# Which score blocks a pair must have free tiles for, in a set-attention kernel followed by an MLP

## The chip, the cores and the metric

The kernel runs on one core of a Trainium2 chip. The metric is the device time of one execution in microseconds. A core has a matmul engine (PE, or TensorE), a vector engine (DVE), a scalar engine (ACT), GpSimd (POOL) and a sync engine (SP), which issues this kernel's DMA transfers. Each engine takes its instructions in the order in which the program issued them and waits on semaphores for what other engines have to deliver.

## The reference

Four batches of 12480 tokens with 128 channels go through an attention in two stages over 32 inducing points, and every token of the result then goes through an MLP of width 2048:

```python
def _attn_ref(x, inducing) -> np.ndarray:
...
    def mab(q, kv):
        s = scale * (q @ kv.transpose(0, 2, 1))
        s = s - s.max(-1, keepdims=True)
        a = np.exp(s)
        a /= a.sum(-1, keepdims=True) + 1e-09
        return a @ kv
    h = mab(I, x)
    return mab(x, h).astype(np.float32)
...
def _moe_ref(x, w_in, w_out) -> np.ndarray:
    h = x @ w_in
    g = h * (1.0 / (1.0 + np.exp(-1.702 * h)))
    return (g @ w_out).astype(np.float32)
```

The first `mab` needs all tokens of a batch before its 32 rows `h` are known. The second scores each token against `h`.

## The kernel before

**Tiling.** A batch is cut into seven parts: six whole super-blocks of 2048 tokens (s = 0 to 5), each of four blocks of 512, and a left-over of 192 tokens (s = 6), two groups of 96. The MLP takes its input block by block. The left-overs of two neighbouring batches make one block together, so there are 98 blocks: 24 of batch 0, one of the left-overs of batches 0 and 1, 24 of batch 1, and the same again for batches 2 and 3. A block has eight **steps** (NG = 8, each for 256 of the 2048 hidden units), 784 steps in all. The block of the first two left-overs begins at step 192, batch 1 at 200, batch 2 at 392, the second pair of left-overs at 584.

**The main loop** (lines 783 to 815) runs over these steps. `first(i)` (line 683) multiplies the stacked softmax weights `st` with `hw`, the product of `h` and `w_in`, into `ph`, and takes the gelu as a sum of two rounded parts, `hi` and `lo`. `second(i, c)` (line 710) multiplies these with the weights `wh` and `wl` into `pso`. The second products follow the first at a distance, `lag`, of 6 to 12 halves. The arithmetic between is on ACT (`g`, some of `hi`) and DVE (`lo`, the rest of `hi`).

**The attention beside it.** While the MLP works on batch b − 1, the attention of batch b is issued in small pieces between its steps. `attention(b)` (line 197) is a generator; the main loop calls `next(rest, None)` once at the end of each step (line 808), so each `yield` in it is a step of waiting. `hop(n)` yields n times, and from batch 1 on `wait(n)` is `hop(n)`, four times without a number. It goes as follows:

- First scores, `first_products` and `first_out`, in pairs of parts: (0, 1), (2, 3), (4, 5), and (6) alone (line 394).
- `maximum`, exponentials, their transposes `aT_of` and the weighted sum `weigh` over all seven parts, which loads the tokens again as `xn` and reloads `xt` for later (lines 405 to 430), then `hT`, the 32 rows (line 441).
- Second scores, `second_products` and `second_out`, in two turns (line 503). For batch 2 the turns are (0, 1), (2, 3) and then (4, 5), (6). For batches 1 and 3, whose left-over is needed first, they are (6, 0), (1, 2) and then (3, 4), (5). At the end of each turn stand its exponentials and `yield LUMP`. The loop answers LUMP by issuing second products until only six halves are held back.

`weights_of(b, s)` (line 534) turns the second exponentials into the stacked weights `st` for the blocks of a super-block, on DVE, POOL and by DMA. `lay_out` (line 775) starts it at a due step, 14 before the first block of the super-block, and earlier where the next one needs it (174 for the left-over of batch 1, 378 for the first super-block of batch 2, 566 for the left-over of batch 3). If the exponentials are not there by then, `lay_out` calls `next(rest)` over and over until they are.

`h_w_in` (line 519) makes `hw` for the next batch in four parts, at steps 186, 188, 190 and 193 for batch 1, 385, 387, 389 and 391 for batch 2, and 578, 580, 582 and 585 for batch 3. It uses the tag `pa`, two PSUM banks, as the scores do.

**The tiles that scores go to.** `take` (line 137) gives a whole super-block a tile from a ring of EB = 9 under tag `e`, for first and second scores alike, and writes `False` for it into the list `held`. A left-over gets a tile of a ring of its own, `e_last`, and no entry. `give_back` sets the entry to `True`: `aT_of` does so for first scores and `weights_of` for second scores. `full(n)` (line 133) asks, for each of the next n takes, whether the entry nine places back is still `False`. Before a pair the generator yields as long as `full(len(pair))` holds (lines 395 and 506). Each batch makes twelve entries: batch 0 has 0 to 5 for first scores and 6 to 11 for second, batch 1 has 12 to 17 and 18 to 23, batch 2 has 24 to 29 and 30 to 35, batch 3 has 36 to 41 and 42 to 47.

Of the kernel before, what the change touches and what calls it, by code (L numbers as in the profile page):

```python
# [55 lines left out]
def set_attention_then_moe(ctx: ExitStack, tc, xT, x, indT, w_in, w_out, outT):  # L56
# [31 lines left out]
    NS = len(sups)  # L88
    EB = NS + 2
# [40 lines left out]
    pace = [0]  # L130
    held = []

    def full(n=1):

        return any(len(held) + k >= EB and not held[len(held) + k - EB] for k in range(n))

    def take(name, s):
        if s == NS - 1:
# [9 lines left out]
    def hop(n=4):  # L148

        for _ in range(n):  # L150
            yield
# [7 lines left out]
    def load_xT(b, s):  # L159
        t0, g, w = sups[s]  # L160
        if g == G:
            t = px.tile([P, SUP], F32, tag="xt", name="xt")
        else:
            t = px.tile([P, g * w], F32, tag="xt_last", name="xt_last", bufs=1)
        nc.sync.dma_start(t[:, 0:g * w], xT[:, b * N + t0:b * N + t0 + g * w])
        xts[b, s] = t
# [30 lines left out]
    def attention(b):  # L197
# [15 lines left out]
        def first_products(s):  # L213
            t0, g, w = sups[s]
            pa = ps_a.tile([P, 512], F32, tag="pa", name="pa")
            xg = xts[b, s][:, 0:g * w]
            if start:
                xg = xg.rearrange("c (k g i) -> c g k i", g=g, i=32)
            else:
                xg = xg.rearrange("c (g t) -> c g t", g=g)  # L220
            for j in range(g):
                pe_.matmul(
                    pa[32 * j:32 * j + 32, 0:w], indT_sb, xg[:, j], start=True, stop=True
                )
            return pa

        def first_out(s, pa):
            t0, g, w = sups[s]
            q = 32 * g
            e, slot = take("s1", s)  # L230
            if start:
                act.copy(e[0:q, 0:w], pa[0:q, 0:w])
                dve.tensor_reduce(mx[0:q, s:s + 1], pa[0:q, 0:w], axis=AX.X, op=ALU.max)
            else:
                dve.tensor_copy(e[0:q, 0:w], pa[0:q, 0:w])
                dve.tensor_reduce(mx[0:q, s:s + 1], e[0:q, 0:w], axis=AX.X, op=ALU.max)
            s1[s] = e, slot
# [65 lines left out]
        def pairs(some):  # L303
            some = list(some)
            return [some[k:k + 2] for k in range(0, len(some), 2)]

        def again(s):

            if s < NS - 1:
                load_xT(b, s)  # L310
# [81 lines left out]
            dve.tensor_add(hu, hu, h2[:, 0:P])  # L392
        else:
            for pair in pairs(range(NS)):
                while full(len(pair)):
                    yield
                pas = [first_products(s) for s in pair]
                yield
                for s, pa in zip(pair, pas):
                    if s + XB < NS:  # L400
                        load_xT(b, s + XB)
                    first_out(s, pa)
                    yield from wait(2)
                yield from wait(2)
# [46 lines left out]
        def second_products(s):  # L451
            t0, g, w = sups[s]
            pa = ps_a.tile([P, 512], F32, tag="pa", name="pa")
            for j in range(g):
                pe_.matmul(
                    pa[32 * j:32 * j + 32, 0:w], hT[:, 0:M], xts[b, s][:, j * w:(j + 1) * w],
                    start=True, stop=True,
                )
            return pa

        def second_out(s, pa):

            t0, g, w = sups[s]
            q = 32 * g
            e, slot = take("e", s)
            k = w // 32
            e = e[:, 0:w].rearrange("p (k m) -> p k m", m=M)
            dve.transpose(e[0:q].rearrange("p k m -> p (k m)"), pa[0:q, 0:w])
            m2 = psm.tile([P, BLK], F32, tag="m2", name="m2")
            dve.tensor_reduce(m2[0:q, 0:k], e[0:q], axis=AX.X, op=ALU.max)  # L470
            yield
            eng = dve if start and s == 0 else nc.gpsimd
            eng.tensor_sub(e[0:q], e[0:q], m2[0:q, 0:k].unsqueeze(2).broadcast_to([q, k, M]))  # L473
            yield
            return e, slot

        def exponentials(s, e):
            q = 32 * sups[s][1]
            act.activation(e[0][0:q], e[0][0:q], AF.Exp, scale=scale)
            es[b, s] = e  # L480
# [22 lines left out]
        for some in (turn[2:],) if start else (turn[0:4], turn[4:]):  # L503
            yield from hop(20 if start else 8)
            for pair in pairs(some):
                while full(len(pair)):
                    yield
                pas = [second_products(s) for s in pair]
                yield
                for s, pa in zip(pair, pas):  # L510
                    if s + XB < NS:
                        again(s + XB)
                    mine[s] = yield from second_out(s, pa)
                yield from wait(2)
            for s in some:
                exponentials(s, mine[s])
            yield LUMP
# [214 lines left out]
    squared = [0]  # L732
    loaded_w = []
    att = attention(0)
    with tc.tile_pool(name="pf", bufs=FB) as pf, tc.tile_pool(name="pw", bufs=2) as pw:
        dec = weights()
# [13 lines left out]
    def attentions():  # L750
        yield from att
        for b in range(1, B):
            while first_block[b - 1, 0] * NG > now[0]:
                yield
            yield from attention(b)

    n = len(work) * NG
# [91 lines left out]
```

## Time and profile before

| | us |
|---|---|
| median of 3 runs | 1657.11 |
| lowest and highest | 1654.92, 1658.01 |
| the profiled execution | 1656.42 |
| its span, from the first to the last instruction | 1654.6 |

The profile is of that one execution. Its page lists busy time by engine, the span in 40 slices, the DMA queues, the chain of work that ended last, and the costliest groups of instructions. Nearly all compute instructions have line 46, the helper that records them, so one goes by the tiles' names: `pa` for scores and small products, `ph` for the first products, `pso` for the second, `e` and `s` for score tiles, `xt` and `xn` for loaded tokens. In the timeline a row has start, duration, engine, line, operation, output and inputs, and in brackets the idle time before it and what ended that. Consecutive `ph` rows on PE mark the steps of the main loop.

### The profile page before, as it was taken

The numbers are of one execution on the slowest core, as the hardware profiler recorded it, in microseconds if no ns is written. First come the engines' busy times: TensorE is split into PE (matmuls) and PEld (weight loads), VectorE is DVE, ScalarE is ACT, GpSimd is POOL, SyncE is SP. The second block draws the span as 40 slices with busy tenths as digits, with TensorE's granted clock in tenths as the row PEclk, the third lists the DMA queues.
The fourth block names the chain that finished last, engine by engine and source line by source line (L and its number), as shares of the span: only waits on it lengthen the run. The fifth ranks groups of instructions, "written<-read, shape, count | busy, mean of one in ns | idle before, by whom it ended". The sixth has DMA issues, their size and how long they took to land.

```text
span 1654.6 us, 21847 instructions
## 1 busy us (share of the span) xinstructions
PE 1595.2 (96%) x7737; PEld 1239.9 (75%) x7737; DVE 1382.3 (84%) x1524; ACT 1326.1 (80%) x1504; POOL 189.8 (11%) x134
## 2 busy tenths in 40 slices
PE   5799999999989999999979999999999999999999
PEld 3577787777667877777747777777766888888887
DVE  7798987888769888788877988878888888888886
ACT  6488888988768888888757887898876988788885
POOL 4311110110301011011020110110122011001100
PEclk9799999999999999999999999999999999999999
DMA  8305102841141110374123201149210111011010
GB/s 333 103 21 189 42 25 58 191 107 51 60 145 70 39 45 26 69 187 98 45 71 133 87 19 39 45 91 217 52 66 22 37 45 42 17 45 45 20 45 20
DMA packets 81947, 126.66 MB, mean 77 GB/s; under 512 B 11632, under 2 KB 50096, under 8 KB 75696
## 3 DMA queue, kind: packets, MB, share of 16 engines
q1 hardware_dynamic: 81840, 125.26, 26.6%
q8 instruction: 63, 1.03, 0.3%
q14 instruction: 44, 0.36, 0.1%
HBM read 74.10 MB, written 25.56 MB: 60 GB/s over the span
## 4 chain that ended last, share of the span: by engine, by line
PE 89%; DVE 5%; ACT 2%; DMA 2%; issue 1%; POOL 1%; SPq 0%; ACTq 0%; DVEq 0%; POOLq 0%
PE pso L46 63%; PE ph L46 22%; PE pa L46 4%; DVE lo L46 2%; DMA xt<-in_xT 2%; DVE e L46 1%; DVE m L46 1%; ACT hi L46 1%; ACT g L46 1%; DVE hw L46 0%; DVE hi L46 0%; ACT L46 0%; DVE t L46 0%; ACT s L46 0%; DVE sm L46 0%
## 5 line engine op out<-in xcount | busy, mean ns | idle before, releaser
L46 DVE TENSOR_TENSOR lo<-g,hi 128x1024 fp32r<-128x1024 f32 (+1 forms) x784 | 976.2, 1256 | 154.2 <-ACT hi L46 141.3
L46 ACT ACTIVATE g<-ph 128x1024 f32<-128x1024 f32 (+1 forms) x784 | 805.1, 1030 | 245.8 <-PE ph L46 138.6
L46 PE MATMUL pso<-hi,wl 128*128 128x512 f32 (+1 forms) x1568 | 626.7, 400 | 0.0
L46 PE MATMUL pso<-hi,wh 128*128 128x512 f32 (+1 forms) x1568 | 618.9, 395 | 0.0
L46 PE MATMUL pso<-lo,wh 128*128 128x512 f32 (+1 forms) x1568 | 618.0, 394 | 0.0
L46 PE MATMUL ph<-st,hw 128*128 128x512 f32 x1536 | 490.9, 401 | 11.1 <-ACT g L46 8.9
L46 ACT ACTIVATE hi<-ph 128x1024 fp32r<-128x1024 f32 x455 | 465.2, 1022 | 0.0
L46 PEld LDWEIGHTS ph<-st,hw 128*128 128x128 f32 x1536 | 284.2, 189 | 99.3 <-issue 16.4
L46 PEld LDWEIGHTS pso<-lo,wh 128*128 128x128 f32 x1568 | 296.0, 189 | 73.0 <-issue 3.7
L46 PEld LDWEIGHTS pso<-hi,wl 128*128 128x128 f32 x1568 | 296.5, 189 | 71.3 <-issue 2.8
L46 PEld LDWEIGHTS pso<-hi,wh 128*128 128x128 f32 x1568 | 296.5, 189 | 70.6
L46 DVE CAST hi<-g 128x1024 fp32r<-128x1024 f32 (+1 forms) x329 | 242.2, 736 | 86.3 <-ACT g L46 85.6
L546 POOL TENSOR_TENSOR e<-e,sm 128x512 f32<-128x512 f32 (+1 forms) x27 | 39.1, 1448 | 1143.5 <-DVE sm L46 898.4
L46 ACT COPY ob<-pso 128x512 f32<-128x512 f32 (+1 forms) x98 | 57.8, 590 | 27.2 <-PE pso L46 27.2
L473 POOL TENSOR_TENSOR e<-e,m 128x512 f32<-128x512 f32 (+1 forms) x27 | 34.8, 1289 | 203.2 <-DVE m L46 203.2
L550 POOL TENSOR_TENSOR e<-e,ah 128x512 f32<-128x512 f32 (+1 forms) x27 | 49.7, 1841 | 2.2
L46 PE MATMUL pa<-xt,indT_sb 128*32 128x512 f32 x192 | 25.7, 638 | 15.9 <-DMA xt<-in_xT 15.9
L46 ACT ACT_TABLE_LOAD x28 | 35.9, 1283 | 4.4 <-issue 3.3
L549 POOL CAST ah<-e 128x512 fp32r<-128x512 f32 (+1 forms) x27 | 34.5, 1277 | 1.7
L46 PE MATMUL pa<-xt,hT 128*32 128x512 f32 x192 | 26.0, 639 | 7.2 <-DVE e L46 4.0
L46 ACT ACTIVATE e<-e 128x512 f32<-128x512 f32 (+1 forms) x28 | 15.2, 576 | 21.6 <-POOL e L473 14.0
L46 PE MATMUL pa<-w_in_sb,hT 128*128 128x512 f32 x24 | 14.0, 669 | 12.1 <-DVE hw L46 8.3
(97 smaller groups left out, 445.1 us busy)
## 6 DMA issues: line engine op xcount, KB each, us to landing
xt<-in_xT SPq DMA_DIRECT2D x48, 1024.0 KB, 7.1
out_T<-ob SPq DMA_DIRECT2D x96, 256.0 KB, 2.0
xn<-in_x SPq DMA_DIRECT2D x72, 256.0 KB, 7.0
st<-ahT SPq DMA_DIRECT2D x192, 64.0 KB, 2.0
st<-alT SPq DMA_DIRECT2D x192, 64.0 KB, 2.0
raw<-in_w_in SPq DMA_DIRECT2D x4, 512.0 KB, 8.9
raw<-in_w_out SPq DMA_DIRECT2D x4, 512.0 KB, 8.3
xt_last<-in_xT SPq DMA_DIRECT2D x4, 96.0 KB, 8.2
```

Of the source, the lines that this page charges most:

```text
L46: return f(*a, **k)
L473: eng.tensor_sub(e[0:q], e[0:q], m2[0:q, 0:k].unsqueeze(2).broadcast_to([q, k, M]))
L546: eng.tensor_mul(e[0:q], e[0:q], sm[0:q, 0:nb].unsqueeze(2).broadcast_to([q, nb, M]))
L549: eng.tensor_copy(ah[0:q, 0:w], e2[0:q])
L550: eng.tensor_sub(e2[0:q], e2[0:q], ah[0:q, 0:w].bitcast(F32))
```

## The change

`full` is given the parts of the pair instead of their number. It counts those that are whole super-blocks and looks at the entries nine places back for so many takes. A pair (6, 0) is asked about one tile instead of two, and (6) alone about none. Both calls, before first scores and before second scores, are changed alike.

```diff
-    def full(n=1):
-
-        return any(len(held) + k >= EB and not held[len(held) + k - EB] for k in range(n))
+    def full(some):
+
+        free = range(len(held) - EB, len(held) - EB + sum(s < NS - 1 for s in some))
+        return any(k >= 0 and not held[k] for k in free)
...
-                while full(len(pair)):
+                while full(pair):
                     yield
                 pas = [first_products(s) for s in pair]
...
-                while full(len(pair)):
+                while full(pair):
                     yield
                 pas = [second_products(s) for s in pair]
```

## The prediction

> **What bounds the kernel now.** I read the page first: the busy shares, then the chain of work that ended last.
>
> ```profile
> span 1654.6 us, 21847 instructions
> ...
> PE 1595.2 (96%) x7737; PEld 1239.9 (75%) x7737; DVE 1382.3 (84%) x1524; ACT 1326.1 (80%) x1504; POOL 189.8 (11%) x134
> ...
> PE 89%; DVE 5%; ACT 2%; DMA 2%; issue 1%; POOL 1%; SPq 0%; ACTq 0%; DVEq 0%; POOLq 0%
> ```
>
> TensorE is busy for 96% of the span and holds 89% of the chain. A change that only moves work can win no more than the time in which PE waits or runs slowly. So the question is where those places are, and whether the moved step touches them. The timeline of PE, followed along the first products (`ph<-st,hw`, one pair of them in each step of the main loop), gives the rhythm. Here are four stretches of it, each around an undisturbed step: a plain step, one with a part of `h_w_in`, one with a pair of scores, one with the left-over scores.
>
> ```profile
> 822.32 0.63 PE L46 MATMUL ph<-st,hw 128*128 128x512 f32 x2
> 824.26 1.92 PE L46 MATMUL pa<-xt,hT 128*32 128x512 f32 x16
> 826.11 0.74 PE L46 MATMUL ph<-st,hw 128*128 128x512 f32 x2
> 828.09 0.63 PE L46 MATMUL ph<-st,hw 128*128 128x512 f32 x2
> ...
> 849.75 0.63 PE L46 MATMUL ph<-st,hw 128*128 128x512 f32 x2
> 851.60 0.63 PE L46 MATMUL ph<-st,hw 128*128 128x512 f32 x2
> 852.07 1.02 PE L46 MATMUL pa<-w_in_sb,hT 128*128 128x512 f32 x2
> 854.31 0.63 PE L46 MATMUL ph<-st,hw 128*128 128x512 f32 x2
> ...
> 882.13 0.63 PE L46 MATMUL ph<-st,hw 128*128 128x512 f32 x2
> 884.09 0.36 PE L46 MATMUL pa<-xt_last,hT 128*32 128x96 f32 x4
> 884.38 0.74 PE L46 MATMUL ph<-st,hw 128*128 128x512 f32 x2
> ```
>
> A plain step lasts 851.60 − 849.75 = 1.85 us. A part of `h_w_in` makes it 2.71 (+0.86). A pair of scores takes 828.09 − 822.32 = 5.77 for two steps, 2.07 above two plain ones, so one whole super-block costs about 1.03. The left-over costs 2.25 − 1.85 = 0.40.
>
> Against these prices I set three stretches of the windows view, one for each of the batches 1, 2 and 3, around the second scores, and two quiet stretches below them. The columns are the stretch, its length, then busy time (and instructions) of PE, PEld, DVE, ACT and POOL, the granted clock, the DMA share and GB/s.
>
> ```profile
> 408.98:464.04 55.06, 48.03 (x211) 32.55 (x210) 43.94 (x54) 35.19 (x41) 15.64 (x13) 0.94 0.16 56
> 828.09:880.26 52.17, 39.88 (x161) 26.36 (x160) 36.74 (x42) 29.75 (x34) 12.15 (x9) 0.93 0.18 59
> 1219.38:1272.97 53.59, 46.60 (x211) 31.41 (x210) 43.53 (x54) 35.15 (x41) 15.64 (x13) 0.97 0.16 57
> 600.00:650.00 50.00, 50.00 (x216) 40.20 (x215) 42.96 (x44) 40.70 (x46) 4.91 (x3) 1.00 0.09 29
> 268.00:345.00 77.00, 77.00 (x441) 61.03 (x440) 60.73 (x63) 70.31 (x85) 5.24 (x3) 1.00 0.69 159
> ```
>
> PE stands idle 7.03, 12.29 and 6.99 us in the three, none in the quiet two, and the clock drops below 1.00 in the three alone. The real loss is larger than the idle time:
> Batch 1 runs 19 steps (35.15), the left-over (0.40), six whole super-blocks (6.2) and three parts of `h_w_in` (2.58), 44.3 in all. It took 55.06: **10.7 lost**.
> Batch 2 runs 15 steps (27.75), two pairs (4.14) and four parts (3.44), 35.3. It took 52.17: **16.8 lost**.
> Batch 3 is the work of batch 1, 44.3. It took 53.59: **9.3 lost**. Together 36.8 us.
>
> What the loss is made of, in the timeline of PE:
>
> ```profile
> 413.14 1.97 PE L46 MATMUL pa<-xt,hT 128*32 128x512 f32 x16 [1.00 <-DVE e L46]
> ...
> 421.72 1.22 PE L46 MATMUL ph<-st,hw 128*128 128x512 f32 x2 [2.70 <-ACT g L46]
> ...
> 454.45 0.73 PE L46 MATMUL ph<-st,hw 128*128 128x512 f32 x2
> 458.24 1.49 PE L46 MATMUL pa<-w_in_sb,hT 128*128 128x512 f32 x2 [3.05 <-DVE hw L46]
> 462.08 0.72 PE L46 MATMUL ph<-st,hw 128*128 128x512 f32 x2
> ...
> 860.10 0.73 PE L46 MATMUL ph<-st,hw 128*128 128x512 f32 x2
> 864.68 1.74 PE L46 MATMUL pa<-w_in_sb,hT 128*128 128x512 f32 x2 [3.85 <-DVE e L46]
> 868.64 0.62 PE L46 MATMUL ph<-st,hw 128*128 128x512 f32 x2
> ...
> 1232.10 0.73 PE L46 MATMUL ph<-st,hw 128*128 128x512 f32 x2 [2.70 <-ACT g L46]
> ...
> 1267.18 1.47 PE L46 MATMUL pa<-w_in_sb,hT 128*128 128x512 f32 x2 [3.05 <-DVE hw L46]
> ```
>
> There are two kinds. First a **burst**: at its due step `lay_out` calls `next(rest)` until the weights of the next batch exist, so both pairs, four `second_out` and the exponentials are issued at once (413.14, 421.72, 1232.10). Then a **collision**: the second turn of pairs, late too, shares the two `pa` banks with `h_w_in` (458.24, 864.68, 1267.18). Both come of one lateness.
>
> **The change, part by part.** Where the lateness comes from shows in two rows, the last first-score pair of batch 1 and its left-over:
>
> ```profile
> 182.19 1.92 PE L46 MATMUL pa<-xt,indT_sb 128*32 128x512 f32 x16
> ...
> 243.55 0.36 PE L46 MATMUL pa<-xt_last,indT_sb 128*32 128x96 f32 x4
> ```
>
> These are 61.4 us apart, 32 steps; the pair itself has 7 yields. For the other 25 steps the generator stands in `while full(len(pair))` for a tile that the left-over never takes. By the yields in the code: pair (4, 5) at step 56, left-over possible at 63; tile 18 − 9 = 9, that of super-block 3 of batch 0, comes back at step 87 (its weights are laid out 14 steps before its first step 96, and 5 steps later it is returned), so the left-over runs at 88. `hT` follows at 166, the second scores would begin at 175, and `lay_out` of (1, 6) is due at 174.
>
> *What is removed:* for a left-over alone the new `full` looks at no tile. Batch 1: 63, `hT` 141, pair (6, 0) at 150, pair (1, 2) at 157, exponentials at 164, ten steps ahead of 174; pair (3, 4) at 173, (5) at 180, done at 185, ahead of `h_w_in` at 186. Batch 2 goes from 288 to 263: pairs at 350 and 357, exponentials 364 (due 378), then 373, 380, done 385, when `h_w_in` starts. Batch 3 goes from 480 to 455 and repeats batch 1 (164 becomes 556, due 566). The bursts go, and the second turn no longer lies among the parts of `h_w_in`. I take the whole 36.8.
>
> *The rule for second scores itself* frees nothing: in the old order pair (6, 0) came at 174, when tile 10 was long back (119). In the new order tiles 10 and 11 are back at 119 and 151, and pair (1, 2) comes at 157; in batch 2 tile 23 is back at 351 and its pair comes at 357. Cost and gain zero, with six steps to spare.
>
> *What moves:* DVE, ACT, POOL and DMA work of batch b stays the same in number; it lies 25 steps (46 us) earlier beside the same steady loop. Three collections of exponentials, one a batch, now return LUMP to the main loop instead of having it swallowed inside `lay_out`, so the loop issues its six held-back halves behind them; these are no extra matmuls. The moved middle part (exponentials, `aT`, `weigh`, loads of `xn` and `xt`) now begins at step 80, just ahead of `weights_of` of super-block 3 at 82, which has DVE and POOL work of its own. Below, this costs nothing, as 268 to 345 has the same work beside super-block 4 with PE at 77.00 of 77.00. Above, it is bounded by a burst's wait each time, 2.70 and about 1.5 of slow clock, 12.6 for three batches. I take 2, near the lower end, because that row shows the very same work.
>
> *What is new:* attention of batch 3 ends seven steps earlier and so begins at step 392 instead of 399, at the first step of a super-block, when SP also issues the last four stack loads. Batch 2 begins at such a step now (200), and its second load comes late:
>
> ```profile
> 487.53 0.62 PE L46 MATMUL ph<-st,hw 128*128 128x512 f32 x2
> ...
> 492.10 1.09 PE L46 MATMUL pa<-xt,indT_sb 128*32 128x512 f32 x8 [2.26 <-DMA xt<-in_xT]
> 493.12 1.22 PE L46 MATMUL ph<-st,hw 128*128 128x512 f32 x2
> 496.58 0.63 PE L46 MATMUL ph<-st,hw 128*128 128x512 f32 x2
> ```
>
> 496.58 − 487.53 = 9.05 where a pair and two steps need 5.77: 3.3 lost. Batch 3 may take from 0 to 3.3; I take 3.3, as the queue has the same order there. Batch 2 keeps its own.
>
> The page "TensorE: Matmul & The Clock Gate" of the Trainium skill (Part 1) lets the clock fall only after an idle window of about 3.4 us. By that, the 2.26 us of the load would cost 2.3 and the sum would be an estimated 1 us better. The trace disagrees: after 2.70 idle the matmuls at 421.72 took 1.22 instead of 0.63, while after 2.70 at 1232.10 they took 0.73, so a shorter wait can cool the array or not.
>
> **Sum:** 36.8 − 2 − 3.3 = 31.5 us off the profiled execution's 1656.42 us (its span 1654.6 and 1.8 around it): 1624.9. That execution lay 0.7 below the median of 1657.11, so I say 1625.5.
>
> **Rivals.**
> *The collision stays.* If the LUMP at 185 or 385 holds ACT just as `h_w_in` needs its copies, the waits at 458.24, 864.68 and 1267.18 remain: 462.08 − 454.45 = 7.63 against 2.71, 4.9 lost, about the same in batch 3, and 868.64 − 860.10 = 8.54 against 2.71, 5.8; 15.6 in all. Saved 36.8 − 15.6 − 3.3 = 17.9: 1639. For it: the two still follow each other closely. Against: with no pair between them, each part of `h_w_in` waits for the bank of the part two before it, four steps old.
> *A larger gain.* The load waits of batches 2 and 3 both vanish and nothing is paid: 36.8 + 3.3 = 40.1, 1617.
> *Nothing changes.* If the second pairs waited instead, for tiles 11 or 23, until step 174 or 378, the bursts would stay: 1657. The spare six steps speak against it.
> *Slower.* SP is one queue in order. The stacks of super-block 3 (steps 90 to 96) now stand behind the moved loads:
>
> ```profile
> xt<-in_xT SPq DMA_DIRECT2D x48, 1024.0 KB, 7.1
> ...
> xn<-in_x SPq DMA_DIRECT2D x72, 256.0 KB, 7.0
> ```
>
> If a stack had to wait for one of each, PE would miss it for 14.1 us and 1.6 of slow clock, 47 for three batches: 47 + 3.3 − 36.8 = 13.5 slower, 1671. It decides from a delay of 11.2 us a batch. Against: the row 268 to 345 has the same loads beside the stacks of super-block 4, DMA share 0.69, and PE never idle.
>
> **How the numbers follow.** Forecast 0.68, with 1618 to 1636 as its own range (the two unknown costs at their ends give 1620 to 1636). Collision stays 0.14 (1636 to 1645). Larger gain 0.08. Nothing 0.04. Slower 0.06. The range 1615 to 1642 takes in the forecast, half of the larger gain and most of the staying collision, 0.82. About 0.2% (3.3 us) is what a measurement of this kernel can tell from no change. Faster is 0.68 + 0.14 + 0.08 = 0.90, same 0.04, slower 0.06.
>
> **What would show it.** In the changed trace the left-over's first scores of batch 1 should start about 13 us after their pair, not 61; the pairs of second scores should lie seven steps apart, each in a step of 3.8 us; the waits of 2.70 for `g` and 3.05 and 3.85 for `hw` and `e` should be gone; a wait for `xt` should stand at step 396. I am wrong if PE waits for `hw` after the LUMP, for `lo` in steps 80 to 96, or for a stack at a step that is a multiple of eight.

## The result, and the profile after

| | median us | lowest to highest | ratio to before, with its 95% interval |
|---|---|---|---|
| before | 1657.56 | 1654.92 to 1659.52 | |
| after | 1632.13 | 1632.03 to 1632.70 | 0.9848, 0.9831 to 0.9865 |

The change makes the kernel 25.4 us faster. The forecast was 1625.5, with a range of 1615 to 1642. The profiled execution after took 1632.70 us. Its page, with the rows that answer to those of before:

```profile
span 1630.9 us, 21863 instructions
...
PE 1591.0 (98%) x7737; PEld 1233.0 (76%) x7737; DVE 1386.9 (85%) x1515; ACT 1331.5 (82%) x1513; POOL 197.9 (12%) x134
```

PE does the same 7737 matmuls and is busy for 98% of a span that is 23.7 us shorter. The busy time itself fell by only 4.2 us, so most of the gain is waiting that went away. The place of it shows when both traces are cut at the same steps. The cuts must lie where the same work is done on either side, so each stretch runs from before the last first scores of a batch to behind its second scores and the first pairs of the next one. Here are windows of the trace before, from step 50 to 250, 250 to 442, 442 to 608 and 620 to 780 (columns as in the prediction):

```profile
170.49:578.10 407.61, 398.30 (x1929) 310.56 (x1928) 342.91 (x379) 334.19 (x378) 43.51 (x31) 0.99 0.29 80
578.10:978.92 400.82, 388.02 (x1855) 298.25 (x1854) 331.68 (x356) 322.56 (x362) 37.22 (x25) 0.99 0.30 80
978.92:1316.34 337.42, 330.22 (x1631) 257.69 (x1630) 282.99 (x314) 279.08 (x318) 38.36 (x28) 0.99 0.28 71
1338.58:1635.11 296.53, 296.53 (x1281) 240.25 (x1280) 256.95 (x255) 244.24 (x266) 19.78 (x12) 1.00 0.12 35
```

The same four stretches of steps after the change:

```profile
170.50:572.70 402.20, 397.97 (x1930) 308.71 (x1928) 343.36 (x375) 336.76 (x381) 45.64 (x31) 0.99 0.30 81
572.70:959.79 387.09, 384.26 (x1855) 296.26 (x1854) 333.67 (x353) 324.45 (x365) 40.97 (x25) 1.00 0.30 83
959.79:1290.27 330.48, 329.28 (x1631) 256.55 (x1630) 284.58 (x311) 280.93 (x321) 40.75 (x28) 1.00 0.29 72
1312.67:1611.34 298.67, 298.67 (x1282) 240.12 (x1280) 257.32 (x255) 244.22 (x266) 19.79 (x12) 1.00 0.12 35
```

The matmul counts agree to one, so the stretches hold the same work. At step 50 both kernels are at 170.5 us. Then the three stretches are 5.4, 13.7 and 6.9 us shorter, 26.1 in all; idle PE in them falls from 9.31, 12.80 and 7.20 us to 4.23, 2.83 and 1.20. From step 608 to the end the kernel takes 340.6 us instead of 338.3 (1630.9 − 1290.27 against 1654.6 − 1316.34): 2.4 come back in a tail whose work the change does not touch (see the rhythm of the tail below). The 26.1 and the 2.4 make the span's 23.7.

What the moved middle of batch 1 costs shows beside this. Both rows are the 64 steps that end with `hT`, first before, at steps 102 to 166, then after, at steps 77 to 141:

```profile
268.55:396.01 127.46, 127.46 (x718) 101.14 (x716) 105.59 (x116) 112.79 (x130) 12.35 (x8) 1.00 0.51 117
```

```profile
222.23:350.66 128.43, 128.29 (x717) 100.87 (x716) 106.71 (x115) 111.05 (x129) 9.89 (x6) 1.00 0.51 116
```

It is 0.97 us dearer at its new place. In batch 2 it is 0.89 (128.39 against 127.50), in batch 3 0.87 (128.38 against 127.51): 2.7 in all. In batch 1 the extra lies in steps 87 to 95.

The early left-over and the second scores that are no longer in a burst, in PE's timeline after:

```profile
197.23 0.36 PE L46 MATMUL pa<-xt_last,indT_sb 128*32 128x96 f32 x4
...
367.34 0.63 PE L46 MATMUL ph<-st,hw 128*128 128x512 f32 x2
...
369.47 1.03 PE L46 MATMUL pa<-xt,hT 128*32 128x512 f32 x6
370.43 0.74 PE L46 MATMUL ph<-st,hw 128*128 128x512 f32 x2
```

The left-over's first scores stand at 197.23 instead of 243.55. Pair (6, 0) of batch 1 is at step 150, alone, and its step lasts 370.43 − 367.34 = 3.09 us without a wait. The waits of 2.70 for `g`, of 3.05 for `hw` and of 3.85 for `e` are gone.

### The profile page after: what moved, and what is told of

Its sections match the earlier page's. It is cut to its first block, busy times and chain, and to the rows that moved or that the text cites. A ratio compares the mean times of both kernels' runs of the same rounds, so it can differ in the third digit from the quotient of the medians.

```text
span 1630.9 us, 21863 instructions
## 1 busy us (share of the span) xinstructions
PE 1591.0 (98%) x7737; PEld 1233.0 (76%) x7737; DVE 1386.9 (85%) x1515; ACT 1331.5 (82%) x1513; POOL 197.9 (12%) x134
## 4 chain that ended last, share of the span: by engine, by line
PE 88%; DVE 4%; ACT 3%; DMA 2%; issue 2%; SPq 1%; POOL 0%; ACTq 0%; DVEq 0%; POOLq 0%
PE pso L46 62%; PE ph L46 22%; PE pa L46 4%; DMA xt<-in_xT 2%; DVE lo L46 2%; ACT g L46 1%; ACT hi L46 1%; SPq L575 1%; DVE sm L46 1%; DVE hi L46 0%; DVE e L46 0%; DVE m L46 0%; DVE hw L46 0%; DVE t L46 0%; ACT s L46 0%
## 5 line engine op out<-in xcount | busy, mean ns | idle before, releaser
L46 ACT ACTIVATE hi<-ph 128x1024 fp32r<-128x1024 f32 (+1 forms) x464 | 474.1, 1022 | 0.0
L46 DVE CAST hi<-g 128x1024 fp32r<-128x1024 f32 x320 | 239.6, 749 | 77.0 <-ACT g L46 76.7
L547 POOL TENSOR_TENSOR e<-e,sm 128x512 f32<-128x512 f32 (+1 forms) x27 | 44.0, 1631 | 1132.8 <-DVE sm L46 1132.8
L474 POOL TENSOR_TENSOR e<-e,m 128x512 f32<-128x512 f32 (+1 forms) x27 | 42.5, 1574 | 180.4 <-DVE m L46 135.8
L550 POOL CAST ah<-e 128x512 fp32r<-128x512 f32 (+1 forms) x27 | 30.3, 1122 | 1.7
L46 PEld LDWEIGHTS pa<-xt,indT_sb 128*32 128x32 f32 x192 | 4.8, 114 | 28.7 <-issue 15.6
```

What stands on the lines that cost most here:

```text
L46: return f(*a, **k)
L547: eng.tensor_mul(e[0:q], e[0:q], sm[0:q, 0:nb].unsqueeze(2).broadcast_to([q, nb, M]))
L550: eng.tensor_copy(ah[0:q, 0:w], e2[0:q])
```

## The experiments

The runs of one group share a chip and their runs of the kernel before. Ratios are to that.

**Which call carries the gain?** In e1 the old rule stays before second scores, in e2 before first scores.

```diff
-                while full(pair):                # e1: the call before second scores
+                while full_old(len(pair)):
...
-                while full(pair):                # e2: the call before first scores
+                while full_old(len(pair)):
```

> The new rule holds for first scores alone; second scores keep the old one. My theory: all of the gain comes from the left-over's first scores, which no longer stand 25 steps before a tile that they never take, so this runs like the changed kernel, 1632 us (1630 to 1635). Rival, after the change's own words: the second scores' waiting counts; then a part of the 25 us is missing here, 1640 us or more.

> The new rule holds for second scores alone. My theory: their tiles were always back in time, so this runs like the kernel before, 1657 us (1654 to 1660). Rival: the second scores' waiting counts; then this is faster than 1652 us.

e1 took 1630.46 us (1629.49 to 1631.55), ratio 0.9843 (0.9828 to 0.9857). e2 took 1658.22 us, ratio 1.0005 (0.9994 to 1.0016). The whole gain comes from the left-over's first scores. The rule before second scores moves nothing: in the order after the change, as before it, their tiles are back in time.

**Bursts or collisions?** e3 keeps the first turn of second scores early and puts only the second turn back to the steps at which it stood before.

```diff
+            late = not start and some[0] != turn[0]
-            yield from hop(20 if start else 8)
+            yield from hop(20 if start else 8 + (9 if b % 2 else 13) * late)
```

> The changed kernel, with the second turn of second scores held back 9 steps (batches 1 and 3) or 13 steps (batch 2), to the steps 182, 386 and 574 at which it stood before; the first turn stays early. Theory of two kinds of loss (bursts and collisions with h_w_in): the bursts stay away, the waits for hw and e at h_w_in come back (4.9 in batches 1 and 3, about 10 in batch 2, less the 4.6 now left in these places, and less the 1.1 load wait of batch 3, whose attention starts later again): about 1647 us (1642 to 1651). Rival, the burst alone was the loss and the collision its echo: 1632 us.

It took 1647.03 us (1646.13 to 1647.58), ratio 0.9942 (0.9927 to 0.9957), the time that was expected. Its PE timeline at step 190:

```profile
450.40 0.73 PE L46 MATMUL ph<-st,hw 128*128 128x512 f32 x2
454.17 1.76 PE L46 MATMUL pa<-w_in_sb,hT 128*128 128x512 f32 x2 [3.04 <-DVE hw L46]
458.13 0.62 PE L46 MATMUL ph<-st,hw 128*128 128x512 f32 x2
```

The wait for `hw` is back, 3.04 where it was 3.05, and the step takes 458.13 − 450.40 = 7.73 where it took 7.63. No burst precedes it. So the collision is a loss of its own. By the medians e3 lies 14.9 us above the changed kernel (1647.03 − 1632.13), but that is not the price of the collisions. Here are the first three of the four stretches in e3:

```profile
169.96:574.12 404.16, 397.67 (x1929) 308.91 (x1928) 343.72 (x377) 335.10 (x380) 45.39 (x31) 0.99 0.30 80
574.12:971.26 397.14, 388.25 (x1855) 297.56 (x1854) 331.14 (x353) 324.17 (x365) 39.17 (x25) 0.99 0.30 81
971.26:1306.06 334.80, 330.41 (x1631) 257.28 (x1630) 283.27 (x312) 279.90 (x320) 40.79 (x28) 0.99 0.29 71
```

They are 2.0, 10.0 and 4.3 us longer than after the change, 16.3 in all. In the same trace the loads at the start of batches 2 and 3, the next question, cost about 2.3 and 1 us less. So the collisions cost 19 to 20 us, and the rest of what the second scores lost before the change was the bursts. That e3's time was met is in part luck: its sum had 15.2 for the collisions (4.9 + 10 + 4.9 − 4.6), and left out the start of batch 2 and a tail that runs 2.1 us quicker.

**The loads at the start of an attention.** After the change, PE waits for `xt` in the first pair of batch 2 and now of batch 3 too:

```profile
477.69 0.62 PE L46 MATMUL ph<-st,hw 128*128 128x512 f32 x2
...
483.24 1.94 PE L46 MATMUL pa<-xt,indT_sb 128*32 128x512 f32 x8 [2.77 <-DMA xt<-in_xT]
485.11 1.22 PE L46 MATMUL ph<-st,hw 128*128 128x512 f32 x2
488.05 1.05 PE L46 MATMUL ph<-st,hw 128*128 128x512 f32 x2
490.45 0.62 PE L46 MATMUL ph<-st,hw 128*128 128x512 f32 x2
...
874.86 1.06 PE L46 MATMUL pa<-xt,indT_sb 128*32 128x512 f32 x8 [0.87 <-DMA xt<-in_xT]
```

The step of batch 2's pair and the two behind it take 12.76 us. Three plain steps and a pair need 7.62, but these three hold three second products fewer (0.70 us), and nine of theirs belong to the left-over block, 384 columns wide, and follow each other at 0.17 us instead of 0.23 (0.52 in all). So they need about 6.4, and 6.4 are lost. In batch 3 the two steps from 870.95 on take 6.87 for 5.77, 1.1 lost. e4 waits five steps more between the loads and that pair.

```diff
                 load_xT(b, s)
                 yield
+            if b > 1:
+                yield from hop(5)
```

> The changed kernel, with five more steps between the loads of xt and the first pair of first scores in batches 2 and 3. The later pairs stand waiting for tiles until steps 256 and 448 anyway, so nothing else moves. Theory: the loads are on the way during those steps, the waits at steps 204 and 396 (6.5 and 1.1 us of lost time with their slow clock) go: 1632.1 - 7.6 = 1624.5 us (1623 to 1627). Rival: the transfer is late because of the queue, not of the start, or other work is crowded instead: 1630 us or more.

It took 1622.51 us (1622.36 to 1624.85), ratio 0.9799 (0.9782 to 0.9815). Its first two stretches, steps 50 to 250 and 250 to 442:

```profile
170.00:565.96 395.96, 394.77 (x1929) 306.98 (x1928) 342.55 (x375) 336.52 (x382) 45.26 (x31) 1.00 0.30 82
565.96:952.20 386.24, 384.52 (x1856) 296.26 (x1854) 332.89 (x353) 324.58 (x365) 40.63 (x25) 1.00 0.31 83
```

They are 6.2 and 0.9 us shorter than after the change, 7.1 where the theory had 7.6, and the clock in the first is back at 1.00. The rest of the 9.6 us lies mostly in the tail, which is the question after this. Repeated as e9 on another chip, e4 took 1625.34 us (1622.70 to 1626.92), ratio 0.9812 (0.9798 to 0.9825).

> e4 unchanged, as the measure for e8 on the same chip: 1622.5 us (1621.5 to 1624).

This median lies above the expected range. The profiled execution of e9, 1622.70 us, is the fastest of its four, and its stretches are those of e4 within 0.3 us; what made the other three longer stays open.

**The rhythm of the tail.** The last rows of the two groups of four above are the same 160 steps, 620 to 780: 296.53 us before and 298.67 after the change, with PE busy in all of it and the clock at 1.00 in both. A plain step lasts 1.853 us in the first and 1.867 in the second. e4's trace has the shorter step (296.54 us). e5 puts one dummy matmul into the loop at step 602, e6 two, e7 one into e4.

```diff
         now[0] = i
+        if i == 602:
+            spin(1)                              # e6: spin(2); e7: this in e4
```

> The changed kernel with one more small matmul (128x128, its result unused) on PE at step 602. In the changed kernel's trace a plain step of the last 180 lasts 1.867 us, in the trace before and in e4 1.853, with PE busy throughout and its clock at 1.00 in all. Theory A: PE runs in one of two rhythms, into which the last interruption sets it; the dummy is a new interruption and can set the other: 1630 us (2.4 less, plus 0.2 for itself) and 1.853 in the trace. Theory B: the rhythm is fixed by the order of instructions or the places of the buffers: 1632.3 us and 1.867.

> As e5, with two dummies. Theory A: either rhythm, 1630 or 1632.5 us, and it need not agree with e5. Theory B: 1632.5 us and 1.867.

> e4 with one dummy matmul at step 602. Theory A: the tail may stay at 1.853 (1622.7 us) or go to 1.867 (1625 us). Theory B: 1.853 and 1622.7 us.

PE's timeline of e5 around the dummy (`spun`), along the first products:

```profile
1271.03 0.63 PE L46 MATMUL ph<-st,hw 128*128 128x512 f32 x2
1272.90 0.63 PE L46 MATMUL ph<-st,hw 128*128 128x512 f32 x2
1274.77 0.63 PE L46 MATMUL ph<-st,hw 128*128 128x512 f32 x2
1276.64 0.38 PE L46 MATMUL spun<-ident 128*128 128x128 f32 x2
...
1278.71 0.63 PE L46 MATMUL ph<-st,hw 128*128 128x512 f32 x2
1280.56 0.63 PE L46 MATMUL ph<-st,hw 128*128 128x512 f32 x2
1282.41 0.62 PE L46 MATMUL ph<-st,hw 128*128 128x512 f32 x2
```

Two steps take 1274.77 − 1271.03 = 3.74 us ahead of the dummy and 1282.41 − 1278.71 = 3.70 behind it, and so it stays: the 160 steps take 296.54. The traces of e6 and e7 show the same, steps of 1.867 ahead of the dummies and of 1.853 behind them. So the dummy changed the rhythm. And e7 was slow up to there, while e4 and e9, with the same instructions up to step 602, were quick. The order of instructions alone (B) does not set the rhythm. A is not shown to the end: all three changes went to the quick rhythm, none the other way. In time, e5 took 1629.80 us (1628.04 to 1632.23), e6 1631.06 (1628.29 to 1631.86) and e7 1623.31 (1622.84 to 1625.09). The medians of e5 and e6 lie 2.3 and 1.1 below that of the changed kernel, but on another chip and with their highest close to it, so the times alone would not show it. Each trace is of one execution; which rhythm the others had is not known.

**A crowd on DVE and POOL.** What is left in the second scores of batch 2 stands at steps 383 and 384. The timeline of after there, DVE, POOL and PE:

```profile
838.90 1.30 POOL L547 TENSOR_TENSOR e<-e,sm 128x512 f32<-128x512 f32 x1 [2.32 <-DVE sm L46]
...
839.34 5.74 DVE L46 TENSOR_TENSOR lo<-g,hi 128x1024 fp32r<-128x1024 f32 x3
...
841.83 2.16 POOL L551 TENSOR_TENSOR e<-e,ah 128x512 f32<-128x512 f32 x1
842.48 0.73 PE L46 MATMUL ph<-st,hw 128*128 128x512 f32 x2 [1.31 <-ACT g L46]
```

Three `lo` take 1.91 us each beside POOL's work instead of the 1.27 that the page of the profile has as their mean, and PE waits. It is so in the whole trace: the 666 `lo` of whole blocks that no POOL instruction overlaps take at most 1.23 us, and the 42 that take more than 1.7 all overlap one. The page "SBUF — State Buffer" of the Trainium skill (Who interferes with whom) has VectorE instructions with two SBUF inputs share a pair of ports with GpSimd, held by one of them at a time; these rows agree, though no run here takes POOL's work away. e8 puts the second turn five steps earlier in e4.

```diff
-            yield from hop(20 if start else 8)
+            yield from hop(20 if start else 8 if some[0] == turn[0] else 3)
```

> e4 with the second turn of second scores five steps earlier in batches 1 to 3 (168, 368 and 560 instead of 173, 373 and 565). Theory: the 2.2 us that batch 2 still loses at steps 383 and 384 come of lo slowed on DVE (about 1.9 us instead of 1.23) while POOL has the subtractions of this turn and weights_of of super-block 0 (step 378) at once, and the 0.6 at steps 183 and 575, 190 and 582 of the turn's nearness to h_w_in; five steps earlier most of it goes: 2 to 4 us less than e4, 1619 to 1621 us. Rival: DVE is short of time there however it is spread; then no difference from e4 (1622.5), or the waits stand at other steps.

e8 took 1620.66 us (1620.36 to 1622.46), ratio 0.9787 (0.9773 to 0.9800), against 1625.34 for e4 on the same chip. Its first three stretches:

```profile
171.54:566.44 394.90, 394.44 (x1930) 307.24 (x1929) 343.40 (x377) 334.94 (x380) 46.49 (x31) 1.00 0.30 82
566.44:950.14 383.70, 383.38 (x1856) 296.58 (x1854) 331.74 (x354) 323.14 (x364) 40.92 (x25) 1.00 0.31 83
950.14:1279.12 328.98, 328.53 (x1631) 256.68 (x1630) 284.64 (x312) 280.03 (x320) 42.24 (x28) 1.00 0.29 73
```

PE is idle for 0.46 and 0.32 us in the first two, where e4 had 1.19 and 1.72. They are 1.1 and 2.5 us shorter than in e4, and the third 1.3 (330.23 there), 4.9 in all, a little more than expected. So the place was right. It does not tell POOL's part from DVE's own load or from the nearness to `h_w_in`. But the tail of the profiled execution has the slow rhythm, 298.67 where e4 has 296.54. So the last run puts the dummy into e8:

> e8 with one dummy matmul at step 602. In e8's trace the turn earlier took 4.2 us off the way to step 602 as against e4, but the tail ran at 1.867 us a step (e4: 1.853) and gave 2.4 back. Theory A (two rhythms, set by the last interruption): the dummy brings the tail to 1.853 as in e5, e6 and e7, 1618.3 us (1617 to 1620). Theory B (fixed by the order of instructions before it): 1.867 and 1620.7 us.

e10 took 1618.20 us (1617.77 to 1619.83), ratio 0.9772 (0.9759 to 0.9786). Here are the first products and the dummy in its timeline:

```profile
1260.92 0.62 PE L46 MATMUL ph<-st,hw 128*128 128x512 f32 x2
1262.77 0.63 PE L46 MATMUL ph<-st,hw 128*128 128x512 f32 x2
1264.62 0.63 PE L46 MATMUL ph<-st,hw 128*128 128x512 f32 x2
1266.48 0.38 PE L46 MATMUL spun<-ident 128*128 128x128 f32 x2
```

The time is the expected one and the tail is quick (296.53 us for the 160 steps), but it was quick ahead of the dummy already: 1264.62 − 1260.92 = 3.70 for two steps. So this trace does not show that the dummy made it quick. e8 has the same instructions up to step 602 and was slow there, as e7 was against e4. All five runs of e10 were shorter than all five of e8; why is open.

e10 is the fastest kernel of this study, 13.9 us below the changed one by the medians and 12.6 by the ratios to the runs of before on each chip. All that it does is move issue times by a few steps and add one matmul.

## Why the prediction was right, and what it mis-sized

- **The cause.** Right. The lateness came from the left-over's first scores, and e1 and e2 show it: all of the gain in the one call, none in the other.
- **The two kinds of loss.** Right. Bursts and collisions were both there, and e3 brings back the collisions alone. The rival "the collision stays" was priced at 15.6 us of loss; e3 has 19 to 20 more than the changed kernel. The price took one step of each batch and left out steps 386 and 389 of batch 2, which lose 2.8 and 2.4 us in e3. The rival did not come true: little crowds the `pa` banks at `h_w_in` any more (0.6 us at steps 190 and 582).
- **What is removed.** Mis-sized. The prediction took out the whole 36.8 us of the second scores. The 26.1 of the three stretches, with the 2.7 of the middle and 3.5 of the new load waits added back, make 32.3. About 4.5 stayed: 2.2 at steps 383 and 384, where POOL and DVE do the second turn and `weights_of` at once, and 0.6 at each of steps 183, 190, 575 and 582. e8 takes about as much away, 4.9, by five steps of distance. The prediction had looked at PE and the `pa` banks for the new places, and not at DVE's and POOL's work there.
- **The new load wait.** Near in sum, wrong in place: 3.5 for 3.3. The whole was given to batch 3, which loses 1.1. Batch 2, which was to keep its own, loses 6.4 where it had lost 4.0. The prediction read those 4.0 as 3.3, because it did not see that the first of the two steps at 487.53 holds three second products fewer than a plain one (0.70 us).
- **What moves.** Near: 2.7 for 2, about 0.9 each time. The extra lies where the middle meets `weights_of` of super-block 3, which starts at step 82 and which the row of 268 to 345 had not held. That this meeting is the cause is argued; no run takes them apart.
- **Not forecast.** The tail's rhythm, 2.4 us in the profiled executions, in steps whose work is the same. Executions of the same instructions had either rhythm, so this term may be chance; the change itself is not shown to cause it.
- **The sum.** The forecast of 31.5 lies 7.8 above the span's 23.7: 4.5 that stayed in the second scores, 0.2 in the loads, 0.7 in the middle and 2.4 in the tail. All but the loads lean to the same side.
- **Nothing changes.** It did not happen; the second pairs of batches 1 and 2 stand at steps 157 and 357, as worked out, and wait for no tile.
- **Slower through SP.** It did not happen; the stacks of super-block 3 came in time.

## What to carry to other kernels

A wait for a resource that the waiting step never takes can lie far from the loss that it causes: here 25 idle steps in a side generator cost nothing where they stood, and showed some 80 steps later as bursts and bank collisions. Follow a late burst back to the first wait that was not needed, and then price the bursts and what they collide with from the plain step of the bound engine. Even where such a kernel keeps PE at 98%, it can pay to move side work by a few steps, away from what shares its engines, or to ask for its data sooner: here the stretches of e4 and e8 became 7.1 and 4.9 us shorter, with no work removed.

## What the runs showed of the hardware

PE has two rhythms for the same stream of eight matmuls a step: 1.867 us (233 ns a matmul) and 1.853 us (232 ns), each held for the last 160 steps and more, with the clock at 1.00 and PE without a gap. In e5, e6 and e7 one or two more matmuls in the stream turned the slow one into the quick one. Executions with the same instructions up to step 602 had either (e4 and e7, e8 and e10). What sets the one or the other stays open.

Whether a wait is followed by a slow clock did not go by its length alone. Before the change the granted clock was 0.50 behind one wait of 2.70 us (421.70 to 424.00) and 1.00 behind another of 2.70 (1232.10 to 1234.07). Around the wait of 2.77 us in the changed kernel, the windows view for PE alone (stretch, length, busy, clock, DMA share, GB/s) reads:

```profile
480.50:483.20 2.70, 0.00 (x0) 0.86 1.01 419
483.20:485.10 1.90, 1.86 (x8) 0.50 1.02 431
485.10:488.05 2.95, 2.95 (x13) 0.50 0.34 144
488.05:490.45 2.40, 2.40 (x9) 0.75 0.24 80
```

So the clock is at half for 4.9 us and comes back in the 2.4 behind, and the start of batch 2, with this wait, costs 6.4. The first row also shows the load that PE waits for: four loads of 1 MB, issued together, were under way, where before the change it was three, and the DMA engines were full at 419 GB/s.
